# Two subtractions moved between the steps of the centroids, and eight token counts read one per block instead of all at once

## The chip, the core and the metric

The kernel runs as one program on one core of one Trainium2 chip. The core has five engines with a sequencer each: TensorE (PE in the profile, its weight loads PEld), VectorE (DVE), ScalarE (ACT), GpSimd (POOL) and SyncE (SP), which here issues nearly all transfers. A trailing q (PEldq, SPq) marks an instruction that the sequencer handles itself, such as a wait, a branch, a register load or the issue of a transfer. The metric is the device time of one execution in microseconds. A difference of about 2% is what a measurement of this kernel can tell from no change.

## What is computed

Three layers follow each other: attention in which a query sees only the keys of its own cluster, a gated normalised MLP on all tokens, and a mixture of eight experts with 1536 tokens, at most 384 to an expert.

```
q_assign = argmax(q_n . c_n)      # nearest of 16 normalised centroids, per head
k_assign = argmax(k_n . c_n)
scores = where(q_assign == k_assign, 0.125 * q @ k.T, -1e9)
x  = softmax(scores) @ v          # 2 batches, 8 heads, 768 tokens, head size 64

h  = x @ w_in;  solu = h * softmax(h)
x  = layernorm(solu) * g_ln @ w_out           # 1536 x 512 -> 1024 -> 512

e  = argmax(x @ w_gate)                       # expert of a token; gate_w its probability
y  = relu(x[tokens of e] @ w1[e]) @ w2[e]     # 8 experts, 512 -> 1024 -> 512
out[token] = gate_w * y                       # tokens above the 384th of an expert stay 0
```

## The kernel before

Values that need more than half precision are held as a high and a low f16 half, and a product is three matmuls: high by high, high by low, low by high.

**Attention.** The 16 heads are taken as 8 pairs. Work is not issued as it stands in the code: each step is given to a planner (`Plan.add`, with engine, cost, due time, a function that issues the instructions, and the names it reads and writes), and `Plan.emit` lists the steps in an order that follows those costs and due times. The function of a step may issue several instructions; they stay together at that place. The wanted semaphores follow from the order of issue. At the start, three things run: the centroids are squared and summed on DVE (`cent`, L275), a power is taken on POOL (L294), DVE finishes the scaling (`cent2_`, L279), PE transposes the result (L298) and DVE copies it into the tile `cbd` in two halves (`cent3`, L285). Beside it the first pair's queries and keys (tile `x32`) are split: ACT writes the high half of each (L322), DVE subtracts to get the low half (L325), into the tile `hl`. The 36 small matmuls L337 to L339 need `cbd` and all four halves; DVE then finds each token's cluster (L346 to L356), PE transposes it (L366) and ACT writes it as `ohT` (L370). SP loads `QK` tiles by transfers from `hl` (L393), from `hr`, a copy of the high halves (L384), and from `ohT` (L389); the score matmuls L446 and L447 read those. In DVE's order between L348 and L351 stands L594, a small subtraction on the gate weights, whose ACT partner L593 waits for the transfer of `wgs` (L591).

**Experts.** After the second layer, tokens lie sorted by expert in the buffer `xs` in HBM; `cnt` holds the 8 token counts and `cnt0` an early version for the first tile. `Experts.run` (L1187) first handles the first 128 tokens of expert 0, called expert -1 in the names (`extra(-1, 0, 2)`, under a branch at L1198 and L1200). Then it reads all eight counts into registers of every engine (L1208, one `TENSOR_LOAD` per count and engine; on SP each is followed by two more register instructions). `first` (L1092 and on) does expert 0's second 128 tokens: two transposed loads of its tokens (`cxT`, L1031) and one for expert 1, 8 x 12 matmuls of 128 columns (L1063 to L1065), the evacuation by ACT (L1076) and DVE (L1077), and 24 matmuls of 512 columns (L1082 to L1084). If expert 0 has more than 256 tokens a third tile follows (branch L1215). `block` then does experts 1 to 7 in turn: it loads the next expert's tokens, runs the first product on 256 or 192 columns by a branch on this expert's count (L1150), the second product of the first 128 tokens (`second`), a branch on the count (L1163) to the second product of the next 128, and inside it a branch to a third tile (L1169). Weight loads (L988) and their splitting by ACT (L991) and DVE (L992) for later experts run along in the blocks.

Of the kernel before, what the change touches and what calls it, by code (L numbers as in the profile page):

```python
# [14 lines left out]
AF = mybir.ActivationFunctionType  # L15
ALU = mybir.AluOpType
# [5 lines left out]
NT = B * S  # L22
DM = H * D
DF = 1024
E = 8
# [49 lines left out]
class Plan:  # L75
# [12 lines left out]
    def add(self, eng, cost, at, fn, reads=(), writes=(), data=0.0, lead=1e9, get=None, put=None):  # L88
        if put is not None:
            put.puts += 1  # L90
        self.todo.append((eng, cost, at, fn, tuple(reads), tuple(writes), data, lead, get, put))
# [104 lines left out]
def plan_attention(tc, plan, ctx, ps, qkT, vP, cent2, cst, cs, X, ident32, ident16):  # L196
    nc, add = tc.nc, plan.add
    pa = ctx.enter_context(tc.tile_pool(name="pa", bufs=1))
    x32 = pa.tile([P, 2, S], F32, tag="x32", name="x32")
    v32 = pa.tile([P, 2, NCH, D], F32, tag="v32", name="v32")  # L200
    hl = ring(pa, "hl", 2, [P, 4, S], F16)
# [47 lines left out]
    for i in range(2):  # L249
        add("sp", 0.0, target(6 * EH - 2.9 + 2.4 * i), lambda i=i: reuse(i),  # L250
            writes=[("QK1", spare[i][0], n) for n in (0, 1, 2, 4, 5)] + [("more", i)])
# [19 lines left out]
    add("pool", 0.1, -101.0, lambda: nc.gpsimd.memset(half, 0.5), writes=["half"])  # L271

    gc = Hold()

    def cent():  # L275
        nc.vector.tensor_tensor(out=sq, in0=cc[:, :D], in1=cc[:, :D], op=ALU.mult)
        nc.vector.tensor_reduce(out=rn, in_=sq, axis=AX.X, op=ALU.add)

    def cent2_():  # L279
        nc.vector.tensor_scalar(out=rn, in0=rn, scalar1=1e-6, scalar2=None, op0=ALU.add)  # L280
        nc.vector.reciprocal(out=rn, in_=rn)
        nc.vector.tensor_scalar(out=rn, in0=rn, scalar1=8.0, scalar2=None, op0=ALU.mult)
        nc.vector.tensor_scalar(out=cc, in0=cc, scalar1=rn[:, 0:1], scalar2=None, op0=ALU.mult)

    def cent3():  # L285
        for j in range(2):
            r = slice(64 * j, 64 * j + 64)
            src = gc.bank[r, :P].rearrange("d (hp j c) -> d hp j c", j=2, c=NC_)[:, :, j, :]
            dst = cbd[r, :, 0, 16 * j : 16 * j + 16]
            nc.vector.tensor_copy(out=dst, in_=src)  # L290
            nc.vector.tensor_tensor(out=cbd[r, :, 1, 16 * j : 16 * j + 16], in0=src, in1=dst, op=ALU.subtract)
# [3 lines left out]
        reads=["half"], writes=["rn"])  # L295
# [3 lines left out]
        reads=["cc", "id32", ("pf", 1)], writes=[gc], get=gc)  # L299
# [8 lines left out]
    def prep(p):  # L308
        hp, b = p % 4, p % 2
        T = 12 * p  # L310

        def at(k):
            return target(T + k)
# [3 lines left out]
        for ts in ((0, 1), (1, 2)) if p == 0 else ((0, 2),):  # L317
            n = ts[1] - ts[0]
            t_ = slice(*ts)
            kx, kh = [("x32", t) for t in range(*ts)], [("hi", b, t) for t in range(*ts)]  # L320
            h_ = hl[b].rearrange("p (t x) s -> p t x s", x=2)[:, t_, 0]
            add("act", 0.64 * n + 0.09, at(-17), lambda h_=h_, t_=t_: nc.scalar.activation(  # L322
                h_, x32[:, t_], AF.Copy, scale=16.0), reads=kx, writes=kh, lead=8)
        for t in range(2):
            add("dve", 0.87, at(-16.5), lambda t=t: nc.vector.scalar_tensor_tensor(  # L325
                out=hl[b][:, 2 * t + 1], in0=x32[:, t], scalar=16.0, in1=hl[b][:, 2 * t], op0=ALU.mult, op1=ALU.subtract),
                reads=[("x32", t), ("hi", b, t)], writes=[("lo", b, t)], lead=8)

        gs, go = Hold(), Hold()
# [13 lines left out]
        def v3():  # L343
# [3 lines left out]
            reads=[gs], writes=["mx"])  # L347
# [343 lines left out]
class Moe1:  # L691
# [18 lines left out]
    def at(self, cost=0.0):  # L710
        t = self.t
        self.t += cost * self.rate
        return t
# [301 lines left out]
class Experts:  # L1015
# [122 lines left out]
            for f, _ in conv[2 * n : 2 * n + 2]:  # L1138
                f()

    def block(self, e, start, r):
        plan = self.plan
        plan.banks = [(0.0, self.two[0])]
        self.hidden(e, 2)
        last, self.later = self.later, []
        if e + 1 < E:
            self.X[e + 1] = self.tiles(self.xk, e + 1, CAP)
            self.rows(e + 1, 0, CAP)
            self.idf(e + 1, 0, CAP)
        with self.tc.If(r > P + HALF) as c:  # L1150
            self.rows2(e, 2 * P, last[:6])
        with c.Else():
            self.rows2(e, P + HALF, last[:6])
        with self.tc.manual_schedule():
            if e + 1 < E:
                plan.add("dve", 0.07, 9.0, lambda: self.ids(e + 1, 0, CAP), writes=[("ids", ((e + 1) % 2, CAP))])
            for n, (_, conv) in enumerate(last[6:]):
                conv(1.2 + 1.2 * (n // 2))
            for n, i in enumerate(range(8 * e + start, min(8 * e + start + 8, 8 * E))):
                c_piece(self.nc, plan, self.piece, i // 8, i % 8, 0.5 + 1.0 * n, self.later)  # L1160
            self.second(e, 0, 1, 0.0, [], CAP)
            plan.emit()
        with self.tc.If(r > P):  # L1163
            with self.tc.manual_schedule():
                for f in range(FC):
                    self.gemm2(self.two[1], e, f, 1)
                self.scale(self.two[1], 1)
                self.put(e, 1, 1)
            with self.tc.If(r > 2 * P):  # L1169
                self.hidden(e, 1)  # L1170
                self.extra(e, 2, 2)
# [13 lines left out]
    def run(self, ctx, start, cnt, cnt0):  # L1185
        tc, nc, plan = self.tc, self.nc, self.plan
        self.xk = ctx.enter_context(tc.tile_pool(name="cx", bufs=2))  # L1187
        self.pools["cs2"] = ctx.enter_context(tc.tile_pool(name="cs2", bufs=LATE))
        one = ctx.enter_context(tc.tile_pool(name="c1", bufs=1))
        self.yo = ring(one, "yo", 3, [P, DM], F32)  # L1190
        self.hr = [ring(one, f"hr{i}", 2, [P, FC, 2 * P], F16) for i in range(2)]
        for h in self.hr:
            for x in h:
                nc.vector.memset(x[:, :, P + HALF :], 0.0)
        self.bank = [plan.banks.pop(0)[1] for _ in range(2)]
        self.four, self.two = [k for _, k in plan.banks[:4]], [k for _, k in plan.banks[4:]]
        plan.MIX, plan.WIN, plan.lean, plan.marks = 0.1, 0.05, {}, ()
        r0 = nc.values_load(cnt0[0:1, 0:1], min_val=0, max_val=NT)  # L1198
        self.hidden(-1, 1)
        with tc.If(r0 > P - 1) as full:  # L1200
            self.extra(-1, 0, 2)
        with full.Else():
            self.rows(-1, 0, P)
            self.idf(-1, 0, P)
            self.ids(-1, 0, P)
            self.extra(-1, 0, 2)
        with tc.manual_schedule():
            regs = [nc.values_load(cnt[0:1, i : i + 1], min_val=0, max_val=NT) for i in range(E)]  # L1208
            for e in range(E):
                if e:  # L1210
                    self.block(e, start, regs[e])
                else:
                    with tc.manual_schedule():
                        self.first(start)
                    with tc.If(regs[e] > 2 * P):  # L1215
                        self.hidden(e, 1)
                        self.extra(e, 2, 2)
# [156 lines left out]
```

## Time and profile before

| | us |
|---|---|
| three runs | 574.69, 565.21, 571.25 |
| median | 571.25 |
| profiled execution, its own time | 569.43 |
| its span, first to last instruction | 567.6 |
| PE busy | 489.6 (86% of the span) |
| DVE / ACT / POOL busy | 411.4 / 364.0 / 277.7 |
| mean granted TensorE clock | 0.971 |

Up to about 387 us the span holds attention and the second layer, and from there the experts. Each row of a timeline is one instruction, or several of a kind merged (x3), with its start and duration; square brackets tell how long its engine was idle before it and what ended that. [...]

### The profile page before, as it was taken

To read this page: it belongs to the slowest core of one execution; us is meant where nothing else is said; L and a number is where in the kernel's file an instruction comes from. 1 tells how busy PE (TensorE), PEld (TensorE's weight loads), DVE (VectorE), ACT (ScalarE), POOL (GpSimd) and SP (SyncE) were. 2 spreads that over 40 slices of the span, in tenths; PEclk is the share of its full clock that TensorE was granted. 3 is DMA by queue.
4 is the path that set the end of the run, shared out by engine and by line. 5 is a ranking of instruction groups with operands and counts; after the bars stand their busy time and mean duration, and the time that the engine had idled before them with its cause. 6 is when DMAs were issued, how large, how long until landed. Compare 5 with 4: busy or idle time off the path is not lost. (4 is left out here: it accounts for less than half of the span.)

```text
span 567.6 us, 13152 instructions
## 1 busy us (share of the span) xinstructions
PE 489.6 (86%) x4921; PEld 320.7 (56%) x4921; DVE 411.4 (72%) x980; ACT 364.0 (64%) x552; POOL 277.7 (49%) x291
## 2 busy tenths in 40 slices
PE   1379889889888798998888999998689999999996
PEld 0256666756565455555455444446664767657753
DVE  5589889999989689998764799994035635455721
ACT  3366789789858698988683688971134715457421
POOL 2046789899969757797883136351001010110210
PEclk9998899899978899999999999999799999999999
DMA  8798887686957999999999889893967792979850
GB/s 230 183 213 184 252 252 210 204 232 180 224 159 188 157 192 182 194 208 218 215 200 196 216 195 217 228 248 77 275 205 232 155 338 55 321 86 332 268 88 17
DMA packets 159268, 113.87 MB, mean 201 GB/s; under 512 B 126480, under 2 KB 134994, under 8 KB 159188
## 3 DMA queue, kind: packets, MB, share of 16 engines
q1 hardware_dynamic: 156660, 106.31, 80.0%
q0 software_dynamic: 2240, 6.32, 3.1%
q8 instruction: 52, 0.85, 0.6%
q14 instruction: 28, 0.23, 0.1%
q10 hardware_dynamic: 288, 0.16, 0.1%
HBM read 51.57 MB, written 16.85 MB: 121 GB/s over the span
## 5 line engine op out<-in xcount | busy, mean ns | idle before, releaser
L409 POOL TENSOR_TENSOR pr<-pf,pr 128x384 f16<-128x384 f32 x168 | 172.0, 1053 | 59.8 <-ACT pr L461 29.5
L1090 POOL DMA_INDIRECT out_dram<-yo,ids x15 | 18.1, 1205 | 145.6 <-ACT yo L1087 43.6
L1063 PE MATMUL psb<-cxT,ah 128*128 128x192 f16 (+2 forms) x288 | 70.3, 252 | 9.3 <-PEq L1169 4.5
L1064 PE MATMUL psb<-cxT,ah 128*128 128x192 f16 (+2 forms) x288 | 70.3, 252 | 1.2 <-issue 1.2
L503 DVE TENSOR_REDUCE mm<-psb 128x1 f32<-128x384 f32 x132 | 67.0, 547 | 6.0 <-PE psb L500 5.6
L1065 PE MATMUL psb<-cxT,al 128*128 128x192 f16 (+2 forms) x288 | 70.2, 252 | 0.0
L537 PE MATMUL psS<-QK 96*128 96x384 f32 x132 | 61.1, 497 | 0.0
L545 ACT ACTIVATE pf<-psS 128x768 f32<-128x768 f32 x66 | 53.1, 805 | 10.5 <-PE psS L537 7.6
L500 PE MATMUL psb<-QK 96*128 96x384 f32 x132 | 47.6, 423 | 14.0 <-DVE mm L503 7.8
L545 ACT ACTIVATE pr<-psS 128x768 f16<-128x768 f32 x66 | 52.6, 804 | 7.7 <-PE psS L537 7.6
L536 PE MATMUL psS<-QK 128*128 128x384 f16 x132 | 46.1, 349 | 1.7 <-ACT pr L545 1.0
L558 PE MATMUL psb<-V,pr 128*128 128x65 f16 x396 | 44.0, 197 | 4.1 <-DVE mm L503 3.6
L1077 DVE SCALAR_TENSOR_TENSOR hr<-psb,hr 128x384 f16<-128x384 f32 (+1 forms) x28 | 16.6, 593 | 39.8 <-ACT hr L1076 39.2
L560 PE MATMUL psb<-V,pr 128*128 128x65 f16 x396 | 43.7, 195 | 1.1 <-POOL pr L409 1.1
L559 PE MATMUL psb<-V,pr 128*128 128x64 f16 x396 | 43.7, 198 | 0.0
L992 DVE SCALAR_TENSOR_TENSOR al<-w,ah 128x1024 f16<-128x1024 f32 x32 | 40.5, 1279 | 3.4 <-ACT ah L991 3.0
L558 PEld LDWEIGHTS <-pr 128*128 128x128 f16 x396 | 37.5, 98 | 7.4 <-issue 2.3
L559 PEld LDWEIGHTS <-pr 128*128 128x128 f16 x396 | 37.8, 99 | 5.6 <-issue 4.7
L500 PEld LDWEIGHTS psb<-QK 96*128 96x128 f32 x132 | 27.7, 220 | 21.5 <-DVE mm L503 13.5
L992 DVE SCALAR_TENSOR_TENSOR bl<-w,bh 128x1024 f16<-128x1024 f32 x32 | 38.4, 1231 | 1.7 <-ACT bh L991 1.7
L1082 PE MATMUL psb<-bh,hr 128*128 128x512 f16 x104 | 39.4, 379 | 0.0
L1083 PE MATMUL psb<-bl,hr 128*128 128x512 f16 x104 | 39.4, 379 | 0.0
(202 smaller groups left out, 1565.1 us busy)
## 6 DMA issues: line engine op xcount, KB each, us to landing
w<-in_w_dram SPq DMA_DIRECT2D x64, 512.0 KB
xs<-X SPq DMA_DIRECT2D x12, 516.0 KB
QK<-hr SPq DMA_DIRECT2D x16, 384.0 KB
QK<-hl SPq DMA_DIRECT2D x32, 192.0 KB
x<-in_qkT_dram SPq DMA_DIRECT2D x7, 768.0 KB
lT<-in_w_in_dram SPq DMA_DIRECT2D x8, 512.0 KB
lT<-in_w_out_dram SPq DMA_DIRECT2D x8, 512.0 KB
v<-in_vP_dram SPq DMA_DIRECT2D x8, 384.0 KB
```

Of the source, the lines that this page charges most:

```text
L409: nc.gpsimd.tensor_tensor(out=out[:, i], in0=a[:, i], in1=b[:, i], op=ALU.subtract)
L500: add("pe", 0.18, at(c - 10 + 0.25 * g), lambda c=c, g=g, w=w: nc.tensor.matmul(w.bank[:, :384], q1[:, c * P : (c + 1) * P], k1[:, g * 384 ...
L503: add("dve", 0.465, at(c - 9.9 + 0.25 * g), lambda c=c, g=g, w=w: nc.vector.tensor_reduce(out=m2[mm][:, c, g : g + 1], in_=w.bank[:, :384] ...
L536: nc.tensor.matmul(o, k2[:, ks], q2[:, qs], start=True, stop=False)
L537: nc.tensor.matmul(o, k1[:, ks], q1[:, qs], start=False, stop=True)
L545: add("act", 0.691, at(k + 0.5), lambda dst=dst, kb=kb: nc.scalar.activation(dst, ps[kb][:, :, :384], AF.Exp, scale=SC), reads=[kb], write ...
L558: nc.tensor.matmul(A, ph[ub][:, c, qs], v[:, j, c, 0:65], start=(c == 0), stop=False)
L559: nc.tensor.matmul(A[:, :64], ph[ub][:, c, qs], v[:, j, c, 65:129], start=False, stop=False)
L992: run("dve", lambda: nc.vector.scalar_tensor_tensor(out=W[e][kl][:, gs], in0=box[0], scalar=64.0, in1=W[e][kh][:, gs], op0=ALU.mult, op1=A ...
L1063: nc.tensor.matmul(o, w["ah"][:, c, fs], x[:, 0, c, a:b], start=(c == 0), stop=False)
L1064: nc.tensor.matmul(o, w["ah"][:, c, fs], x[:, 1, c, a:b], start=False, stop=False)
L1065: nc.tensor.matmul(o, w["al"][:, c, fs], x[:, 0, c, a:b], start=False, stop=(c == KC - 1))
```

## The change

The ACT steps L322 and DVE steps L325 of the first pair are no longer steps of their own (their functions issue nothing); the four functions are kept in a list, `split`. `cent` issues the two ACT instructions ahead of its own two; `cent2_` issues the first subtraction ahead of its four instructions, `cent3` the second one ahead of its four. The other pairs are as before. The planner still sees the same steps with the same costs and names, so it puts all steps in the order in which they stood. In the expert part, the counts of experts 0 and 1 are read after `first`, and in block e the count of expert e + 1 after the second product of the first 128 tokens, ahead of the branch L1163.

```
     def cent():
+        for f in split[:2]:
+            f()
         nc.vector.tensor_tensor(out=sq, in0=cc[:, :D], in1=cc[:, :D], op=ALU.mult)
...
     def cent2_():
+        split[2]()
         nc.vector.tensor_scalar(out=rn, in0=rn, scalar1=1e-6, scalar2=None, op0=ALU.add)
...
     def cent3():
+        split[3]()
         for j in range(2):
...
-            add("act", 0.64 * n + 0.09, at(-17), lambda h_=h_, t_=t_: nc.scalar.activation(
-                h_, x32[:, t_], AF.Copy, scale=16.0), reads=kx, writes=kh, lead=8)
+            fn = lambda h_=h_, t_=t_: nc.scalar.activation(h_, x32[:, t_], AF.Copy, scale=16.0)
+            if p == 0:
+                split.append(fn)
+            add("act", 0.64 * n + 0.09, at(-17), fn if p else lambda: None, reads=kx, writes=kh, lead=8)
...
-            add("dve", 0.87, at(-16.5), lambda t=t: nc.vector.scalar_tensor_tensor(
-                out=hl[b][:, 2 * t + 1], in0=x32[:, t], scalar=16.0, in1=hl[b][:, 2 * t], op0=ALU.mult, op1=ALU.subtract),
+            fn = lambda t=t: nc.vector.scalar_tensor_tensor(
+                out=hl[b][:, 2 * t + 1], in0=x32[:, t], scalar=16.0, in1=hl[b][:, 2 * t], op0=ALU.mult, op1=ALU.subtract)
+            if p == 0:
+                split.append(fn)
+            add("dve", 0.87, at(-16.5), fn if p else lambda: None,
                 reads=[("x32", t), ("hi", b, t)], writes=[("lo", b, t)], lead=8)
...
-    def block(self, e, start, r):
+    def block(self, e, start, r, count):
...
             self.second(e, 0, 1, 0.0, [], CAP)
             plan.emit()
+        if e + 1 < E:
+            count(e + 1)
         with self.tc.If(r > P):
...
-            regs = [nc.values_load(cnt[0:1, i : i + 1], min_val=0, max_val=NT) for i in range(E)]
+            regs = []
+
+            def count(e):
+                regs.append(nc.values_load(cnt[0:1, e : e + 1], min_val=0, max_val=NT))
+
             for e in range(E):
                 if e:
-                    self.block(e, start, regs[e])
+                    self.block(e, start, regs[e], count)
                 else:
                     with tc.manual_schedule():
                         self.first(start)
+                    count(0)
+                    count(1)
                     with tc.If(regs[e] > 2 * P):
```

The line numbers of the changed kernel are higher: L325 becomes L332, L1163 becomes L1175, L1215 becomes L1233, and the reads are at L1223. On DVE, at the start, this stands in a row before (`hl` and `x` are the first pair's tiles, `pf` and `mm` hold the centroids, `psb` is a PSUM bank):

```order
L280 TENSOR_SCALAR mm<-mm 128x1
L281 RECIPROCAL mm<-mm 128x1
L282 TENSOR_SCALAR mm<-mm 128x1
L283 TENSOR_SCALAR pf_163<-pf_163,mm 128x128
L301 CAST tie_145<-cs 128x16
L1263 CAST tri_64<-cs 128x128
L290 CAST cbd<-psb_72 64x4x16
L291 TENSOR_TENSOR cbd<-psb_72,cbd 64x4x16
L290 CAST cbd<-psb_72 64x4x16
L291 TENSOR_TENSOR cbd<-psb_72,cbd 64x4x16
L596 TENSOR_SCALAR gs<-gs 128x8
L325 SCALAR_TENSOR_TENSOR hl_132<-x_130,hl_132 128x768 x2
```

And this in the changed kernel:

```order
L332 SCALAR_TENSOR_TENSOR hl_132<-x_130,hl_132 128x768
L284 TENSOR_SCALAR mm<-mm 128x1
L285 RECIPROCAL mm<-mm 128x1
L286 TENSOR_SCALAR mm<-mm 128x1
L287 TENSOR_SCALAR pf_163<-pf_163,mm 128x128
L306 CAST tie_145<-cs 128x16
L1281 CAST tri_64<-cs 128x128
L332 SCALAR_TENSOR_TENSOR hl_132<-x_130,hl_132 128x768
L295 CAST cbd<-psb_72 64x4x16
L296 TENSOR_TENSOR cbd<-psb_72,cbd 64x4x16
L295 CAST cbd<-psb_72 64x4x16
L296 TENSOR_TENSOR cbd<-psb_72,cbd 64x4x16
```

The two subtractions that stood behind the centroids' copies stand now ahead of `cent2_` and ahead of the copies; the rest of DVE keeps its order, and so do ACT and SP up to the experts.

On PE, between expert -1's last matmul and expert 0's first in `first` (`ah`, `al` are halves of the first weights, `cxT` the tokens), this stands before:

```order
L1084 MATMUL psb_4713<-bh_4726,hl_-1_5672 128x512
L1200 UNCONDITIONAL_BRANCH
L1063 LDWEIGHTS ah_4724
L1208 TENSOR_LOAD cnt x8
L1063 MATMUL psb_4710<-cxT_6049,ah_4724 128x128
```

And in the changed kernel:

```order
L1094 MATMUL psb_4713<-bh_4726,hl_-1_5672 128x512
L1212 UNCONDITIONAL_BRANCH
L1073 LDWEIGHTS ah_4724
L1073 MATMUL psb_4710<-cxT_5937,ah_4724 128x128
L1074 LDWEIGHTS ah_4724
```

The eight register loads are gone from there. On PE at the end of `first`, and then in block 1 behind the second product of the first 128 tokens, the changed kernel has:

```order
L1094 MATMUL psb_72<-bh_4726,hl_5947 128x512
L1223 TENSOR_LOAD cnt x2
L1233 COMPARE_AND_BRANCH
...
L1094 MATMUL psb_75<-bh_5028,hr_5652 128x512
L1223 TENSOR_LOAD cnt
L1175 COMPARE_AND_BRANCH
L1092 LDWEIGHTS hr_5651
```

Two loads stand now ahead of the branch behind `first`, and one ahead of the branch L1163 in each of blocks 1 to 6; on the other four engines the loads moved to the same two places.

## Rows read from the trace of the kernel before

**Rows 1.** The page, busy time, share of the span and instructions of PE.
```profile
PE 489.6 (86%) x4921; PEld 320.7 (56%) x4921; DVE 411.4 (72%) x980; ACT 364.0 (64%) x552; POOL 277.7 (49%) x291
```
**Rows 2.** Timeline of the start: start, duration, engine, line, operation, out<-in, [idle<-releaser].
```profile
4.47 0.84 ACT L322 ACTIVATE hl<-x 128x768 f16<-128x768 f32 x1 [1.54 <-DMA x<-in_qkT_dram]
...
5.51 0.15 DVE L280 TENSOR_SCALAR mm<-mm 128x1 f32<-128x1 f32 x1 [0.76 <-POOL mm L294]
...
6.09 0.29 DVE L283 TENSOR_SCALAR pf<-pf,mm 128x128 f32<-128x128 f32 x1
...
8.09 1.82 DVE L325 SCALAR_TENSOR_TENSOR hl<-x,hl 128x768 f16<-128x768 f32 x2
...
14.04 0.19 DVE L594 SCALAR_TENSOR_TENSOR wgl<-wgs,wgh 128x32 f16<-128x32 f32 x1 [1.88 <-ACT wgh L593]
```
**Rows 3.** Timeline of the start: transfers that SP issues, and who waits.
```profile
9.94 1.31 SPq L393 DMA_DIRECT2D QK<-hl  x2
...
17.68 2.49 SPq L389 DMA_DIRECT2D QK<-ohT  x4
...
23.91 0.66 PE L447 MATMUL psS<-QK 96*128 96x384 f32 x1 [5.66 <-DMA QK<-ohT]
```
**Rows 4.** Stretches of the start: length, busy per engine, PE clock, DMA share, GB/s.
```profile
2.00:14.00 12.00, 1.93 (x37) 1.38 (x37) 6.84 (x18) 4.32 (x6) 2.18 (x10) 1.00 0.96 265
14.00:25.00 11.00, 2.37 (x10) 1.31 (x10) 4.52 (x10) 3.54 (x5) 0.00 (x0) 1.00 0.94 218
```
**Rows 5.** Line L1208: engine, operation, ns min/median/max, first and last start in us.
```profile
L1208 SPq TENSOR_LOAD <-cnt x8: 261/264/543, 387.7 to 392.0; - x8
...
L1208 PEldq TENSOR_LOAD <-cnt x8: 300/307/690, 398.8 to 402.2; - x8
```
**Rows 6.** Timelines of PE, PEld and SP around the same loads.
```profile
384.33 1.25 SPq L1031 DMA_TRANSPOSE cxT-1_5556<-xs  x1
...
387.58 0.22 PE L1063 MATMUL psb<-cxT-1_5556,ah 128*128 128x128 f16 x1 [0.36 <-DMA cxT-1_5556<-xs]
...
395.41 1.70 SPq L1031 DMA_TRANSPOSE cxT<-xs  x1
...
398.79 0.10 PEld L1063 LDWEIGHTS <-ah 128*128 128x128 f16 x1 [1.01 <-PE psb L1084]
...
402.55 0.27 PE L1063 MATMUL psb<-cxT,ah 128*128 128x128 f16 x1 [4.28 <-issue]
```
**Rows 7.** Stretches of expert -1, the gap, `first` in two parts, and block 1.
```profile
387.58:398.27 10.69, 10.69 (x120) 7.58 (x120) 3.19 (x12) 1.59 (x3) 1.96 (x2) 1.00 0.27 78
398.27:402.55 4.28, 0.01 (x1) 0.10 (x1) 0.00 (x0) 0.60 (x1) 0.97 (x1) 0.88 0.83 161
402.55:408.39 5.84, 5.84 (x56) 5.81 (x56) 0.00 (x0) 0.40 (x1) 0.00 (x0) 0.50 1.11 305
408.39:416.02 7.63, 7.63 (x67) 4.54 (x65) 1.67 (x5) 0.80 (x2) 0.00 (x0) 1.00 1.06 389
416.49:436.35 19.86, 18.62 (x144) 12.46 (x144) 11.48 (x13) 10.29 (x14) 2.94 (x2) 1.00 0.57 155
```
**Rows 8.** Four lines on PE's sequencer, ns and starts in us; block 1's second product.
```profile
L1200 PEldq COMPARE_BRANCH x2: 86/195/304, 387.3 to 394.6; - x2
...
L1198 PEldq TENSOR_LOAD <-cnt x1: 498/498/498, 386.7 to 386.7; - x1
...
L1215 PEldq COMPARE_BRANCH  x1: 2877/2877/2877, 412.3 to 412.3; - x1
...
L1163 PEldq COMPARE_BRANCH  x7: 70/70/3377, 427.3 to 557.9; - x7
...
425.83 0.38 PE L1082 MATMUL psb<-bh,hr 128*128 128x512 f16 x1
```
**Rows 9.** Waits of PE from 398 us to the end: total, times, longest.
```profile
PE psb L1063 <- PEq L1169: 4.5, 5, 1.0
...
PE psb L1064 <- issue: 1.2, 1, 1.2
```

More of the change, by code (lines that the diff above doesn't have):

```diff
@@ L273, in plan_attention @@
     gc = Hold()
+    split = []
     def cent():
+        for f in split[:2]:
+            f()
         nc.vector.tensor_tensor(out=sq, in0=cc[:, :D], in1=cc[:, :D], op=ALU.mult)
```

## The prediction

> **What bounds the kernel now.** I read the page first. PE is busy 86% of the span and no other engine is above 72% [rows 1], so time is to be had mostly where PE stands still. Then I went to the two places of the change, with the timeline, the stretches and the waits.
>
> At the start the reader is to see two chains that end in transfers. DVE's chain goes from the centroids to the two subtractions at 8.09 us and on to the clusters, but then DVE stands 1.88 us until 14.04, because L594 waits for ACT's L593, which waits for a transfer [rows 2]. PE's first large matmul L447 stands 5.66 us, until 23.91, for a transfer from `ohT` that SP issued from 17.68 on [rows 3]. And from 2 to 25 us the DMA engines are 94 to 96% busy [rows 4]: the transfers stand in a full queue, and what is issued earlier does not land earlier.
>
> At the beginning of the experts the reader is to see PE's largest gap of the expert part, 4.28 us from 398.27 to 402.55, put down to "issue", that is, to nothing that the profile shows as a wait [rows 6]. The line of the register loads explains it: PE's eight loads start from 398.8 to 402.2 [rows 5]. The weight load that precedes them in program order ran at 398.79 [rows 6], and it stands behind PE's wait for the tokens. A second pair of rows says the same: the earlier transposed load of 128 tokens, issued at 384.33, let PE start at 387.58, 3.25 us later, and this one was issued at 395.41, which gives 398.66 [rows 6]. So the tokens were there at about 398.8, and the eight loads held PE for 402.55 - 398.85 = 3.70 us. [...]
>
> From there to the end PE is the bound: it waits for five gaps of at most 1.0 us behind L1169, one of 1.2 us in block 1, and for little else [rows 9]. What PE wins in `first` therefore moves the rest of the program, if nothing else comes late.
>
> **The change part by part.**
>
> *The subtractions.* New order on DVE, from [rows 2]: the first high half is ready at 4.47 + 0.84 = 5.31; the subtraction takes 1.82 / 2 = 0.91, so until 6.2. The four steps of `cent2_` took from 5.51 to 6.38, 0.87, and now end at 7.1, 0.7 later than before. From there to the subtractions, with PE's transpose and the four copies, it took 6.38 to 8.09, 1.71; with the second subtraction in it and nothing overlapped that ends at 7.1 + 1.7 + 0.9 = 9.7. The small matmuls so have both operands at 9.7 at the latest, in place of 9.91 (8.09 + 1.82); the low halves are complete at some 8.4, behind two short casts, 1.5 us earlier. Both run into what is late next. The clusters stop at L594, 14.04, whatever comes before it. The transfers from `hl`, issued at 9.94 [rows 3], can go about 1.4 us earlier, but into the full queue. The bounds of this part are a gain of 1.5 us, if the queue passed all of that lead on, and 0; a loss is excluded, since both operands of the small matmuls are ready sooner. I take 0, because L594's wait and the DMA share both say that the next stop does not move.
>
> *The eight loads go from the front of `first`.* PE starts at about 398.85: **-3.7 us**. DVE's, ACT's and POOL's loads lay in their own idle time, and SP's ran from 387.7 to 392.0 [rows 5], before it could issue the tokens at 395.41 [rows 6]; they give nothing.
>
> *The clock.* PE's idle time before `first` shrinks from 4.28 to about 0.6 us. Behind the gaps of 1.0 and 1.2 us [rows 9] the clock stayed at 1.00: block 1 with its 1.2 us gap shows it [rows 7]. [...] What that is worth needs no formula: expert -1 has the same 96 + 24 matmuls and took 10.69 us at full clock, while `first` took 5.84 + 7.63 = 13.47 us [rows 7]: **-2.8 us**. The bounds are 0 and -2.8.
>
> *Two loads behind `first`.* One load costs PE (402.55 - 398.79) / 8 = 0.47 us with what lies between two of them [rows 5, 6], so two cost 0.94. Before, PE's sequencer reached the branch L1215 at 412.3, 3.7 us ahead of the end of the matmuls at 416.02, but the branch took 2.88 us, to 415.2 [rows 7, 8]: 0.8 us of the lead was left, which would hide nearly all of it. Against this, block 1 then stood 1.2 us for "issue" [rows 9], which looks as if its instructions came late behind that branch, and a later branch makes them later. The ends are 0.1 and 0.94; I take **+0.9**.
>
> *One load in each of blocks 1 to 6.* In block 1 the second product starts at 425.83 and the branch behind its 24 matmuls was executed at 427.3 [rows 8]. The block's two second products fill 425.83 to 436.35 [rows 7, 8], so the first ends at about 431.1. The sequencer is thus 3.8 us ahead, and a load of 0.3 to 0.7 us lies in that lead: **0** for PE. The load of L1198 shows that a register load does not wait for the array to empty: it ran at 386.7 for 0.5 us [rows 8], up to the time when PE went on to expert -1's matmuls at 387.58, and the rest of that gap belongs to a transfer [rows 6]. If the lead were gone, the cost would be 6 x 0.47 = 2.8 us. On SP a load costs (392.0 - 387.7) / 7 = 0.61 us [rows 5] in front of the next expert's tokens; those are needed a block, some 20 us, later [rows 7].
>
> [...]
>
> *Sum.* 0 - 3.7 - 2.8 + 0.9 + 0 = -5.6 us, against the profiled execution's 569.43: 563.8. That execution is 1.8 us under the median of the three runs, 571.25, which the same sum takes to 565.6. I forecast between the two, **564.7**.
>
> **The rivals.**
>
> *The gap stays cold or refills.* PE starts at 398.85, but its instructions come late, as they did in block 1 for 1.2 us [rows 9]; the eight loads had given them time to come. Or the clock falls anyway. Without the clock's part the gain is 3.7 - 0.9 = 2.8, and the time 571.25 - 2.8 = 568.4 by the median. For it: the jump over the other side of the branch L1200 lies right before. Against it: PE's sequencer went through the last branch of L1200 at 394.6 [rows 8], and had until 398.8 to get what follows. [...]
>
> *The loads in the blocks are not hidden.* If PE has no lead left at L1163, six loads cost 2.8 us and the two behind `first` 0.9: the gain is 6.5 - 3.7 = 2.8, again 568.4. The row at 427.3 speaks against it.
>
> *Slower than before.* Place: the branch L1163 in blocks 1 to 6. If a load waits until the array is empty, PE loses the load, 0.47, then a branch and restart, as behind L1169 up to 1.0 us, and the wait for instructions seen once in block 1, 1.2 us [rows 9]: 2.7 us a block, 16.2 in six, and 0.9 behind `first`, against 6.5 won: 571.25 + 10.6 = 581.9. It decides once a block costs more than (6.5 - 0.9) / 6 = 0.9 us. The load of L1198, which ran to within half a microsecond of running matmuls, speaks against it.
>
> *The start does gain.* If the full queue is not what holds L447, up to 1.5 us come on top: 571.25 - 7.1 = 564.2 by the median, 562.3 by the profiled execution.
>
> **How the numbers follow.** The forecast has a chance of 0.62, the cold or late start 0.12, unhidden loads 0.10, the slower case 0.04, a gain at the start as well 0.12. The three runs of the kernel before span 565.2 to 574.7, so a single median can lie 4 us off for that alone. The range takes in the gaining cases at a fast median, 562.3 - 5, and the two cases at 568.4 with 2 us more: **557 to 570.5**. About 2%, 11.4 us, is what a measurement of this kernel can tell from no change. The forecast is 1.0 to 1.2% below, so within 2% is by far the likeliest, 0.83. Faster by over 2% needs both gains and a favourable spread, 0.14; slower by over 2% needs the slower case nearly in full, 0.03.
>
> **What would show it.** In the changed kernel's profile: PE's gap before `first` is 0.5 to 0.7 us and ended by the transfer of `cxT`, and the clock is 1.00 through it; `first` takes 10.7 us; the gap between `first` and block 1 is 0.5 to 1.5 us, and the loads stand there; no new gap of PE at the six places in the blocks; L447 starts again at about 23.9 us, and DVE's wait at L594 grows to about 2.4 us. I would be wrong if the time from PE's start in block 1 to the end were longer than before, if the clock fell in `first` all the same, or if L447 started more than a microsecond earlier.

## The result, and the profile after

| | before | after |
|---|---|---|
| median of 19 runs each, us | 569.50 | 565.06 |
| lowest and highest | 564.13, 574.69 | 558.37, 569.93 |
| profiled execution (its span), us | 569.43 (567.6) | 565.73 (563.8) |
| mean granted TensorE clock | 0.971 | 0.969 |

The ratio is 0.9903, with a 95% interval from 0.9875 to 0.993: 5.5 us of 569.5. It leaves out executions more than 1.5% above the fastest of their kernel, so it is not the quotient of the medians in the table, which differ by 4.4 us (0.992). Either is less than the 2% that a measurement of this kernel can tell from no change, though the interval leaves out 1. Two later measurements of the same kernel gave 0.9949 (0.9917 to 0.9981) and 0.9893 (0.9818 to 0.9967). The forecast was 564.7 us, 5.6 us less.

The timeline of PE around `first` and the start of block 1, after; columns as in [rows 6]:

```profile
398.70 0.22 PE L1073 MATMUL psb<-cxT,ah 128*128 128x128 f16 x1 [0.50 <-DMA cxT<-xs]
...
409.88 0.26 PE L1073 MATMUL psb<-cxT,ah 128*128 128x192 f16 x1 [0.47 <-PEq L1233]
...
413.15 0.34 PE L1074 MATMUL psb<-cxT,ah 128*128 128x192 f16 x1 [2.03 <-issue]
```

The 4.28 us gap of [rows 6] is 0.50 us and ends with the tokens' transfer. The stall in block 1, 1.2 us in [rows 9], is 2.03 us. In the timeline of the kernel before it stands here:

```profile
418.73 0.26 PE L1064 MATMUL psb<-cxT,ah 128*128 128x192 f16 x1 [1.24 <-issue]
```

The stretches after, columns as in [rows 7], are expert -1, the gap, `first` in two parts, block 1, and the two stretches of [rows 4]:

```profile
387.50:398.20 10.70, 10.70 (x120) 7.60 (x120) 3.20 (x12) 1.60 (x3) 1.96 (x2) 1.00 0.28 77
398.20:398.70 0.50, 0.00 (x0) 0.03 (x1) 0.00 (x0) 0.46 (x1) 0.00 (x0) 1.00 0.31 46
398.70:404.54 5.84, 5.84 (x99) 5.60 (x100) 0.69 (x1) 1.01 (x3) 0.97 (x1) 1.00 1.13 224
404.54:409.40 4.86, 4.86 (x23) 2.01 (x21) 1.00 (x3) 0.32 (x1) 0.00 (x0) 1.00 0.97 352
409.88:432.18 22.30, 20.27 (x144) 13.94 (x144) 11.76 (x14) 10.28 (x14) 2.34 (x2) 0.92 0.92 226
2.00:14.00 12.00, 1.57 (x37) 1.22 (x37) 8.07 (x22) 5.05 (x6) 2.17 (x10) 1.00 0.93 282
14.00:25.00 11.00, 5.19 (x18) 3.46 (x19) 5.77 (x11) 4.39 (x5) 0.00 (x0) 1.00 0.73 206
```

In the first 5.84 us of `first` PE does 99 matmuls at clock 1.00, where it did 56 at 0.50 [rows 7]; the whole takes 10.70 us, not 13.47. Block 1 takes 22.30 us, not 19.86, and its clock is below 1.00: half speed came after the stall, for 3.41 us:

```profile
413.18:416.59 3.41, 3.41 (x22) 3.23 (x23) 0.73 (x2) 1.43 (x2) 0.00 (x0) 0.50 1.07 400
```

The account of the two traces, from PE's start on expert -1 to its last matmul (174.35 us before, 170.71 after):

| stretch | before | after | difference |
|---|---|---|---|
| gap before `first` | 4.28 | 0.50 | -3.78 |
| `first` | 13.47 | 10.70 | -2.77 |
| gap before block 1 | 0.47 | 0.48 | 0 |
| block 1 | 19.86 | 22.30 | +2.44 |
| from there to the end | 125.57 | 126.03 | +0.46 |

The sum is -3.65 us, and the profiled executions differ by 3.70; expert -1 begins at 387.50 against 387.58, so nothing came from the start.

Waits of PE from 389 us on, after, columns as in [rows 9]:

```profile
PE psb L1073 <- PEq L1181: 3.2, 4, 0.9
PE psb L1074 <- issue: 2.0, 1, 2.0
PE psb L1073 <- issue: 1.4, 1, 1.4
PE psb L1073 <- DMA cxT<-xs: 0.5, 1, 0.5
PE psb L1073 <- PEq L1233: 0.5, 1, 0.5
```

And the register loads on PE, after, columns as in [rows 5]:

```profile
L1223 PEldq TENSOR_LOAD <-cnt x8: 302/306/322, 405.7 to 535.0; - x8
```

No matmul of a second product (L1092 to L1094) waits at all: the eight loads, 0.30 us each, show no gap of their own. The start, after, beside [rows 2] and [rows 3]:

```profile
5.32 0.96 DVE L332 SCALAR_TENSOR_TENSOR hl<-x,hl 128x768 f16<-128x768 f32 x1 [0.83 <-ACT hl L327]
...
7.18 0.95 DVE L332 SCALAR_TENSOR_TENSOR hl<-x,hl 128x768 f16<-128x768 f32 x1
...
12.60 0.19 DVE L604 SCALAR_TENSOR_TENSOR wgl<-wgs,wgh 128x32 f16<-128x32 f32 x1 [1.24 <-ACT wgh L603]
...
21.09 0.66 PE L457 MATMUL psS<-QK 96*128 96x384 f32 x1 [4.89 <-DMA QK<-ohT]
```

The subtractions stand where they were put, and PE's first large matmul starts 2.8 us earlier than at 23.91 [rows 3]. Whether that is the change's doing is the first question.

### The profile page after: what moved, and what is told of

Its sections match the earlier page's. It is cut to its first block, busy times and chain, and to the rows that moved or that the text cites. A ratio compares the mean times of both kernels' runs of the same rounds, so it can differ in the third digit from the quotient of the medians.

```text
span 563.8 us, 13152 instructions
## 1 busy us (share of the span) xinstructions
PE 489.6 (87%) x4921; PEld 319.3 (57%) x4921; DVE 415.3 (74%) x980; ACT 364.1 (65%) x552; POOL 277.0 (49%) x291
## 4 chain that ended last, share of the span: by engine, by line
DMA 30%; DVE 28%; PE 18%; issue 14%; ACT 3%; POOL 3%; SPq 2%; POOLq 0%; another core or an unknown queue 0%; ACTq 0%; DVEq 0%
DMA out_dram<-yo,ids 19%; DVE mm L513 7%; DMA x<-in_qkT_dram 2%; DVE wf L626 2%; PE psb L510 2%; DVE hl L332 2%; DMA pr<-pn 2%; DVE wf L629 2%; DMA wT<-wol 2%; DMA QK<-ohT 1%; DVE mm L460 1%; PE psS L456 1%; PE psS L457 1%; DVE wf L623 1%; DMA xs<-ys,si 1%
## 5 line engine op out<-in xcount | busy, mean ns | idle before, releaser
L1073 PE MATMUL psb<-cxT,ah 128*128 128x192 f16 (+2 forms) x288 | 68.6, 249 | 5.6 <-PEq L1181 3.2
L1074 PE MATMUL psb<-cxT,ah 128*128 128x192 f16 (+2 forms) x288 | 68.6, 249 | 2.0 <-issue 2.0
L1075 PE MATMUL psb<-cxT,al 128*128 128x192 f16 (+2 forms) x288 | 68.5, 249 | 0.0
L547 PE MATMUL psS<-QK 96*128 96x384 f32 x132 | 62.4, 507 | 0.0
L1097 ACT ACTIVATE yo<-psb 128x512 f32<-128x512 f32 x16 | 9.6, 597 | 47.9 <-PE psb L1094 22.9
L1086 ACT ACTIVATE hr<-psb 128x384 f16<-128x384 f32 (+1 forms) x28 | 14.6, 521 | 38.6 <-PE psb L1075 38.6
```

The source lines that it names most:

```text
L547: nc.tensor.matmul(o, k1[:, ks], q1[:, qs], start=False, stop=True)
L1073: nc.tensor.matmul(o, w["ah"][:, c, fs], x[:, 0, c, a:b], start=(c == 0), stop=False)
L1074: nc.tensor.matmul(o, w["ah"][:, c, fs], x[:, 1, c, a:b], start=False, stop=False)
L1075: nc.tensor.matmul(o, w["al"][:, c, fs], x[:, 0, c, a:b], start=False, stop=(c == KC - 1))
```

## Experiments

**Theory A**: the gain is PE's gap before `first` and the half clock behind it; the subtractions give nothing. **Theory B**: the subtractions gain at the start as well. A second question came with the trace: what is block 1's stall, which in these two traces grew and, with the half clock behind it, took back 2.4 us?

### Each part alone

`only_loads` is the kernel before with the part of the diff on `count`; `only_subs` is the kernel before with the part on `split`.

```
only_loads:  - regs = [nc.values_load(...) for i in range(E)]
             + regs = []; count(0), count(1) behind first; count(e + 1) in block e
only_subs:   + split: the two ACT and two DVE functions issued in cent, cent2_, cent3
```

> The kernel before with the loads' part of the change alone; the subtractions stand as before. Theory A: the whole gain of the change, 4 to 6 us, ratio 0.990 to 0.993; PE's gap in front of `first` about 0.5 us, `first` 10.7 us at clock 1.00, a stall of about 2.0 us in block 1 some 6.6 us behind the branch after `first`. Theory B: 2 to 4 us, ratio 0.993 to 0.996, since the start gives the rest.

> The kernel before with the subtractions' part of the change alone; the eight loads stand in front of `first` as before. Theory A (the gain comes from PE's gap in front of `first` and the half clock behind it): no gain beyond 0.5 us, ratio 0.999 to 1.001; PE's gap in front of `first` is again about 4.3 us with `first` in part at clock 0.50. Theory B (the two subtractions gain at the start, and the transfers in front of L447 land earlier for that reason): 1.5 to 3 us less, ratio 0.995 to 0.997, and `L447` starts by 21 to 22 us as in the changed kernel.

`only_loads`: ratio 0.9854 (0.9794 to 0.9913). `only_subs`: 0.9985 (0.9951 to 1.002). The stretch of `first` in the trace of `only_loads`:

```profile
396.76:407.46 10.70, 10.70 (x120) 7.59 (x120) 1.69 (x4) 1.36 (x3) 0.97 (x1) 1.00 1.06 274
```

Its first large matmul, in the timeline:

```profile
20.13 0.66 PE L447 MATMUL psS<-QK 96*128 96x384 f32 x1 [5.17 <-DMA QK<-ohT]
```

And the timeline of `only_subs`, the same matmul and the first one of `first`:

```profile
20.80 0.66 PE L457 MATMUL psS<-QK 96*128 96x384 f32 x1 [6.17 <-DMA QK<-ohT]
...
400.23 0.26 PE L1073 MATMUL psb<-cxT,ah 128*128 128x128 f16 x1 [4.46 <-issue]
```

Without the moved subtractions the matmul also starts at 20.1 us, and at 20.6 and 20.5 in `eight_pinned` and `busy_gap` below, which leave them where they were as well; with them moved it starts between 19.6 and 21.4 in ten traces. The 23.9 us of the trace before was that execution's, not the kernel's. The loads carry the gain, somewhat more of it than expected, with an interval that reaches into the expected 0.990 to 0.993. For the subtractions the interval leaves room for a gain of 0.5% or a loss of 0.2%, and 0.15% of gain is what was seen. Theory A holds. Of theory B the reason falls, since L447 does not start earlier for the subtractions; a small gain is not excluded. In the traces expert -1 begins at 385.6 to 388.5 us in the four with the subtractions where they were and at 380.6 to 387.5 in the ten with them moved, and no run shows why.

### What a load costs: its number or its place

`eight_pinned` keeps all eight loads where the kernel before has them and adds one matmul behind them. Before, PE's order was weight load (which waits for the tokens), eight loads, matmul; now the eight loads come ahead of that wait.

```
  regs = [nc.values_load(cnt[0:1, i : i + 1], ...) for i in range(E)]
+ nc.tensor.matmul(self.four[3], self.H[-1][0][:, 0], self.W[0]["ah"][:, 0, :512], ...)
```

> The kernel before, all eight counts read in front of `first` as there, with one such matmul behind the eight loads; nothing else of the change. Theory W: the loads run while the array works on expert -1, PE's gap in front of `first` shrinks from 4.3 to 0.5 to 0.9 us, the clock stays at 1.00 in `first`, and the total is 3 to 6 us under the kernel before, as much as the whole change brings, ratio 0.990 to 0.995. Theory L: the gap stays near 4 us and the time within 1 us of the kernel before.

Ratio 0.9881 (0.9815 to 0.9947), a little more gain than expected; the changed kernel, measured beside it, had 0.9893 (0.9818 to 0.9967). The loads on PE, as in [rows 5]:

```profile
L1208 PEldq TENSOR_LOAD <-cnt x8: 300/306/317, 396.0 to 398.8; - x8
```

PE's first matmul of `first` in the timeline, and the stretch of `first`:

```profile
400.16 0.22 PE L1063 MATMUL psb<-cxT,ah 128*128 128x128 f16 x1 [0.64 <-DMA cxT<-xs]
```

```profile
400.16:410.89 10.73, 10.70 (x120) 7.61 (x120) 1.69 (x4) 1.19 (x2) 0.94 (x1) 1.00 1.05 253
```

All eight loads ran while the array was still on expert -1, and cost PE nothing. What made them cost 3.7 us was that they stood behind the wait for the tokens. Theory W holds, L falls, and by the ratios one matmul gives about the change's whole gain. That trace itself does not show the gain in time: its expert part takes 174.26 us against 174.35 before, since a stall of 2.87 us in block 1, another of 2.38 later and half speed for 3.41 us behind each took back what the gap and `first` had won.

### The clock

`busy_gap` is the same with two matmuls of 512 columns behind each load, so that PE is never idle there.

```
  for i in range(E):
      regs.append(nc.values_load(...))
+     for _ in range(2):
+         nc.tensor.matmul(self.four[3], ...)
```

> The kernel before, with two matmuls of 512 columns into an unused bank behind each of the eight register loads in front of `first`, so that PE works in the gap and is held up as long as before. Theory A (the idle time halves the clock, and the half clock costs 2.8 us): the clock is 1.00 through `first`, which takes 10.7 us instead of 13.5, and the total is 2 to 3 us less than the kernel before, if the matmuls hide under the loads; PE's start in `first` moves by less than 1 us. Rival (the clock falls for another reason, as the matmuls of `first` set in): 0.50 for some 6 us again, and the same time as before or more.

The ratio is 1.0006 (0.9965 to 1.0047), so the expected total did not come. The gap (second row) and `first` (third), and block 1 (fourth):

```profile
387.05:397.70 10.65, 10.65 (x121) 7.81 (x122) 3.21 (x12) 1.62 (x3) 1.96 (x2) 1.00 0.25 73
397.70:401.04 3.34, 3.34 (x17) 1.47 (x15) 0.00 (x0) 0.60 (x1) 0.97 (x1) 1.00 0.70 125
401.04:411.75 10.71, 10.71 (x121) 7.61 (x119) 1.50 (x4) 1.19 (x2) 0.00 (x0) 1.00 0.99 311
414.61:434.39 19.78, 19.78 (x144) 13.73 (x144) 11.67 (x14) 10.12 (x13) 1.52 (x1) 0.93 0.97 184
```

The array was kept from `first` for 3.34 us, but by matmuls and not by idleness, and `first` took 10.71 us at clock 1.00: the 2.8 us of the clock come from the idle gap. Up to the end of `first` the run is 3.74 us ahead of the kernel before (24.70 against 28.44 us from PE's start on expert -1). Then PE stood 2.86 us before block 1, where the branch L1150 takes 2.61 us, and 1.71, 1.44 and 2.07 us for "issue" later on, where the kernel before has no gap over 1.24 us [rows 9]. Its code is 32 instructions longer there; the next experiments say why that matters.

### Where the two loads stand

`two_before` reads counts 0 and 1 ahead of `first`, `loads_mid_first` between its two products.

```
two_before:       + count(0); count(1)      loads_mid_first, in first():
                    self.first(start)       + add("pe", 0.01, t - 0.7,
                  - count(0); count(1)      +     lambda: (count(0), count(1)), ...)
```

> The changed kernel, with the counts of experts 0 and 1 read ahead of `first`, where all eight stood before. Theory A: PE's gap in front of `first` grows from 0.5 to 1.2 to 1.5 us (two loads at 0.41 to 0.47), the clock stays at 1.00 behind it, block 1's stall is back to about 1.2 us, and the total is within 1 us of the changed kernel, ratio 0.988 to 0.992. Theory C (any register load in front of `first` makes PE wait for something else, as instructions, and not for its own duration): the gap stays near 4 us and the ratio near 0.998 to 1.000.

> The changed kernel, with the counts of experts 0 and 1 read between the first and the second product of `first` in place of behind it, so that PE's sequencer reaches the branch behind `first` without two loads in front of it. Theory A1 (block 1's stall ends a fixed 6.4 to 6.6 us behind that branch, because its instructions come late): the branch runs 0.6 to 0.8 us earlier, the stall in block 1 is 1.2 us again in place of 2.0, the clock stays at 1.00 in block 1 and block 1 takes about 19.9 us in place of 22.3: 0.8 to 2.5 us less than the changed kernel, a ratio of 0.986 to 0.989 against the kernel before. Theory A2 (the stall has nothing to do with the loads, and the longer one was chance): same as the changed kernel, 0.990, and a stall of 1.2 to 2.0 us that does not follow the branch.

`two_before`: 0.9936 (0.99 to 0.9972), within 0.2% of the expected range; PE's gap is 1.74 us, more than the 1.2 to 1.5 expected but far from 4, so theory C falls, and block 1 has no stall at all. `loads_mid_first`: 0.9949 (0.9911 to 0.9986), not the gain that A1 expected. Its branch behind `first`, and then block 1 in the timeline:

```profile
L1232 PEldq COMPARE_BRANCH  x1: 4301/4301/4301, 402.0 to 402.0; - x1
```

```profile
412.44 0.34 PE L1074 MATMUL psb<-cxT,ah 128*128 128x192 f16 x1 [4.44 <-issue]
```

The branch was reached earlier, as wanted, but took 4.30 us, and the stall grew to 4.44. A stall 6.5 us behind the branch (theory A1) is refuted here, 10.5 us, and by `two_before`, where none came. The length varies, the place does not: in `loads_mid_first`, as in the changed kernel, it is after 13 matmuls of block 1.

### The stall is a page of instructions that comes late

The trace has the transfers of the instruction queue q8. In the changed kernel, in the 0.1 us from 404.3 and the 0.1 us from 410.7 (packets, MB, and the whole time that the packet took as a share of 16 engines' 0.1 us, so 94.0% is 1.50 us):

```profile
q8 instruction: 1, 0.02, 94.0%
...
q8 instruction: 1, 0.02, 66.2%
```

Those two packets, of 16,384 bytes, end at 405.86 and 411.81. The branch behind `first` ends at 407.23, 1.37 us after the first; block 1's stall ends at 413.15, 1.34 us after the second. From 34.28 to 364.85 us of the trace before, 26 packets of q8 start while PE takes 3312 matmuls and as many weight loads: an estimated 255 instructions to a packet, if all are PE's. Theory P is the author's reading of these times: a packet is a page of PE's code, and behind the branch PE stands until the page that comes next is there. If this is it, moving the code against the pages must move the stall. `pad48` does that and nothing else; `mid_pad48` adds the same to `loads_mid_first`.

```
  with full.Else():                 # not executed with these inputs
      ...
+     for _ in range(24):
+         nc.tensor.matmul(self.bank[0], ...)      # 48 instructions on PE
      self.extra(-1, 0, 2)
```

> The changed kernel with 48 instructions of PE (24 matmuls) added in the side of expert -1's branch that isn't executed: nothing more is computed, but all of PE's code behind it lies 48 instructions further on. Theory P (block 1's stall is a page of instructions that comes late: in the changed kernel the packets of the instruction queue q8, 16 KB or 256 instructions each, end 1.4 us before the branch behind `first` ends, and again before the stall ends; the stall lies at a page's end, 13 matmuls into block 1, and the next page is asked for only when the branch has been taken): the stall 13 matmuls into block 1 is gone; the branch behind `first` takes 0.2 to 0.7 us as its page was asked for earlier; a wait, if any, stands at the very start of block 1, at L1160's branch, and is between 0.5 and 3 us, with a packet of q8 ending 1.4 us before its end. Total within 2 us of the changed kernel. Theory F (block 1's instructions come a fixed 6.5 us behind that branch, wherever the code lies): a stall of about 2.0 us, 13 matmuls into block 1, as before.

> As the last one, with the counts of experts 0 and 1 read between the two products of `first`. Theory P: the branch behind `first` is reached some 7.0 us behind PE's start in `first`, 0.8 us earlier than with the loads behind the second product, and the wait at the start of block 1 is up to 0.8 us shorter: 0 to 2 us. Total 1 to 2.5 us under the changed kernel of the same call. Theory F: the stall stays 13 matmuls into block 1 and is 1.2 us.

> The changed kernel once more, on the chip and in the rounds of the two before it. Both theories: 0.990 of the kernel before, within 0.003. Theory P: block 1's stall lies again 13 matmuls into the block, and its length, 2.0 us before, may be anything from 0 to 4.5 us, since the packet of q8 waits 1.2 to 3.6 us among the other transfers; it ends 1.4 us behind that packet's end. Theory F: 2.0 us again.

> The changed kernel once more, for the comparison with the two in this call: 0.990 to 0.995 of the kernel before, block 1's stall 13 matmuls into the block and 1.5 to 2.0 us long, the expert part 169 to 171 us.

`pad48`: 0.9982 (0.9945 to 1.0018). `mid_pad48`: 0.9915 (0.9864 to 0.9965). `after_again`, beside them: 0.9949. So `pad48` is within the 2 us expected, and `mid_pad48`, expected 1 to 2.5 us under the changed kernel, is not clearly so: its ratio is lower by 1.9 us, but its median over all executions is 569.34 against 567.49. In `pad48` the branch behind `first` and the branch at the head of a block, by their lines, and block 1's first matmul in the timeline:

```profile
L1235 PEldq COMPARE_BRANCH  x1: 437/437/437, 401.5 to 401.5; - x1
...
L1160 PEldq COMPARE_BRANCH  x9: 73/418/3312, 404.6 to 545.0; - x9
```

```profile
407.95 0.34 PE L1073 MATMUL psb<-cxT,ah 128*128 128x192 f16 x1 [3.56 <-issue]
```

The stall has left its place behind 13 matmuls and stands at the head of the block, in the branch L1160, which took 3.31 us instead of 0.22; it ends 1.38 us behind the end of a q8 packet (406.51). That is theory P's picture, and F is refuted. The size that P expected did not come: 3.56 us, and 4.34 in `mid_pad48`, where at most 3 and 2 were expected.

The other traces show the same shift in small steps. The stall stands after 13 matmuls of block 1 in all six traces that have one there and two loads on PE ahead of block 1; after 12 in `two_pinned` below, which has two instructions more (a matmul and its weight load); after 10 in the kernel before and `only_subs`, with eight loads, six instructions more; and after 9 in `eight_pinned`, eight more. Every two instructions ahead of it bring the stall one matmul, which is two instructions, nearer to the block's head.

A stall's end goes with the packet's, 1.24 to 1.79 us behind it in this table, and the packet starts 1.15 to 3.56 us after the branch:

| kernel | branch behind `first` ends | next q8 packet starts (after) | ends | stall ends (after) | stall |
|---|---|---|---|---|---|
| before | 415.19 | 416.34 (1.15) | 417.42 | 418.73 (1.31) | 1.24 |
| only_subs | 412.67 | 415.25 (2.58) | 416.34 | 418.13 (1.79) | 3.17 |
| two_before | 405.39 | 407.78 (2.39) | 408.89 | | none |
| changed | 407.23 | 410.75 (3.52) | 411.81 | 413.15 (1.34) | 2.03 |
| after_again | 407.07 | 410.40 (3.33) | 411.44 | 412.68 (1.24) | 1.50 |
| after_third | 403.47 | 406.94 (3.47) | 408.06 | 409.34 (1.28) | 2.87 |
| only_loads | 405.26 | 408.68 (3.42) | 409.80 | 411.22 (1.42) | 2.04 |
| loads_mid_first | 406.26 | 409.82 (3.56) | 410.93 | 412.44 (1.51) | 4.44 |
| pad48 | 401.94 | 405.40 (3.46) | 406.51 | 407.95 (1.44) | 3.56 |
| mid_pad48 | 400.93 | 404.32 (3.39) | 405.43 | 406.86 (1.43) | 4.34 |

In all thirteen traces with such a stall (four of them are not in the table) the packet moves 1.15 to 3.75 us after the branch, takes 1.0 to 1.1 us, and PE goes on 1.2 to 1.8 us later. In `two_before` the page came early enough for PE not to notice: the packet ended at 408.89, and PE's first matmul of block 1 started at 408.94. In the changed kernel the wait is some 2.3 us longer than in the one trace of the kernel before; `only_subs`, with all loads where they were, has 2.58 and a stall of 3.17, so two traces cannot say that the change made the stall grow. The stretches of that wait, before and after:

```profile
415.19:416.34 1.15, 0.83 (x4) 0.20 (x2) 0.00 (x0) 0.28 (x1) 0.00 (x0) 1.00 0.84 335
```

```profile
407.23:410.75 3.52, 3.05 (x22) 1.66 (x20) 0.00 (x0) 0.60 (x1) 0.44 (x1) 1.00 1.03 386
```

DMA is busier in it (0.84 and 1.03, 335 and 386 GB/s): `first` ends earlier, so the branch falls into the transfers of the next weights. In the other twelve traces the share is 0.91 where the wait is 2.39 us (`two_before`) and 0.99 to 1.08 where it is 2.58 to 3.75. That these transfers hold the page up is argued from such rows; no run took them away.

`after_third` shows the spread: 174.86 us for the expert part, against 170.71 and 169.33 in the other two traces of the same kernel, with stalls of 2.87, 2.33 and 1.88 us, where 169 to 171 us and one stall of 1.5 to 2.0 were expected.

### Two further runs

`two_pinned` is `two_before` with one matmul behind the two loads.

> The changed kernel with the counts of experts 0 and 1 read ahead of `first`, as in the run that read two there, and one matmul (512 columns, on operands that have long been there, into an unused bank) behind them, so that the loads stand ahead of PE's wait for the tokens and not behind it. Theory W (a register load costs PE time only where it stands behind a wait; ahead of one it is done while the array still works): PE's gap in front of `first` is 0.5 to 0.9 us and no longer 1.7, the branch behind `first` comes some 7.0 us after PE's start there, block 1's stall is 0 to 1.5 us, and the expert part (from PE's start on expert -1 to its end) takes 167.5 to 169 us against 168.75 with two loads behind the wait and 170.7 and 169.3 in two traces of the changed kernel; total 1 to 2 us under the changed kernel of this call. Theory L (each load costs its 0.4 us wherever it stands on PE): a gap of 1.2 to 1.7 us again, and the same total as the changed kernel.

PE's gap before `first` is 0.60 us instead of 1.74, so theory W holds there as well; but block 1's stall is 2.91 us (the packet waited 3.63), the expert part 174.12, and the ratio 0.9878 (0.9772 to 0.9985). The expected total was wrong, and no version here is clearly better than the changed kernel.

`four_per_block` issues `count(e + 1)` four times in each of blocks 1 to 6.

> The changed kernel with three more reads of the count in each of blocks 1 to 7, so four loads (three in block 7) stand ahead of the branch L1175 where one stood. Theory A (the loads lie in the 3.7 us that PE's sequencer is ahead of the array there): four loads take 1.7 us of the lead, PE shows no gap between the two second products in any block, and the expert part is within 1 us of the changed kernel's 169.3 to 170.7, but for stalls at the pages' ends, which lie elsewhere. Rival (a load holds the array up): a new gap of 1.2 us or more in each of seven blocks, 8 us or more in all.

This run misses its question. Its trace has 26 loads on SP, but on PE again eight, and 18 semaphore instructions in place of the others, so PE's price for more loads was not tried. What it shows is small: no second product waits.

## Why the prediction was right, and where it was not

**The eight loads, -3.7 us: right**, measured -3.78. The reason given was right too: they stood behind the wait for tokens that were there. `eight_pinned` makes it sharper: with all eight ahead of that wait the gap is 0.64 us, so the wait in front of them is nearly the whole price.

**The clock, -2.8: right.** `first` took 10.70 us at clock 1.00, measured -2.77, and `busy_gap` ties it to the idle gap.

**The two loads behind `first`, +0.9: mis-sized.** The sentence was that the branch's lead "would hide nearly all of it", against a later branch and a later stall, so that the ends were 0.1 and 0.94. The gap stayed at 0.48 us, so the loads themselves cost nothing. The branch was not later either: it ended 2.2 us ahead of the end of `first`, and before 0.8 us ahead [rows 7, 8]. The stall did grow between the two traces, by 0.79, but not by the loads' length: the page of instructions waited 3.52 us instead of 1.15. And the prediction had no term for the clock behind it: half speed for 3.41 us, about 1.65 more. The term was +2.44 in that trace; how much of it is the change's doing stays open, as `only_subs` shows a stall of 3.17 us with half speed behind it and no load moved. The full clock that was expected in `first` held there and was lost in block 1.

**The block loads, 0: right as far as tried.** No gap at the six places; single loads took 0.30 us, as those in a row. So the rival of loads that are not hidden did not come.

**The subtractions, 0: right within 0.5%**, though the sign named for being wrong appeared: the first large matmul came 2.8 us earlier. `only_loads` has that too, without them, and the lead was gone by 387.5 us. DVE's wait at L604 was 1.24 us and not the 2.4 predicted, since ACT's L603, which waits for the transfer of `wgs`, started at 12.34 us and not at 13.78. That what is issued earlier does not land earlier, the premise of the 0, no run shows: in the trace after, the transfers from `ohT` were issued at 16.24 us and not at 17.68, and L457, which waits for one, came earlier with them.

**The sum.** -5.6 was forecast, -5.5 is the ratio's, and the two traces alone give -3.7. With the other traces, the expert part takes 174.35 and 178.04 us with the eight loads behind the wait (before, `only_subs`), and 170.71, 169.33, 174.86 and 171.75 with the loads moved (three of the changed kernel, `only_loads`): 4.5 us less on average. The agreement is in part luck and closer than the parts deserve: three traces of the changed kernel differ by 5.5 us in the expert part, and the repeated ratios run from 0.989 to 0.995.

## What to carry to other kernels

Look at what stands ahead of a register load on its engine: here eight were free ahead of a wait (PE's gap was 0.64 us in `eight_pinned`), and behind it they cost 3.7 us and 2.8 us of half clock after it (a gap of 4.28 us). Where a stall is put down to "issue" behind a branch, look for the packets of the instruction queue before moving work about to shorten it: here it ended 1.2 to 1.8 us behind one, and 48 instructions that never run moved it by 13 matmuls (`pad48`). A change that pulls a stage forward pulls its branches with it, here into transfers with a DMA share of 1.03 in place of 0.84; that the page waited for those was argued and not tested, but some of the gain may be lost so. Where executions of one kernel differ by more than the change is worth, account for several traces of each kernel.

## What was not expected of the hardware

Where a page of instructions was missing, PE went on 3.5 to 6.2 us after the branch behind which it was needed (packet of 16,384 bytes 1.15 to 3.75 us after it, then 1.0 to 1.1, then 1.2 to 1.8). 48 instructions that never run moved a stall of PE from the middle of a block to its head.

With PE's stalls in block 1 of 2.0 us and more the granted clock was 0.50 for 3.4 us (2.03, 2.04, 2.86, 2.87 twice, 3.17, 3.42) or 6.8 us (2.91, 3.56, 4.34, 4.44); with those of 1.24 and 1.50 it stayed at 1.00. The length of a stall alone does not tell it: later in the expert part the clock stayed at 1.00 behind gaps of 1.98, 2.06, 2.07 and 2.30 us (`two_before`, `only_loads`, `busy_gap`, `two_pinned`) and was 0.50 for 3.4 us behind those of 2.15, 2.17, 2.33 and 2.38 (`mid_pad48`, `pad48`, `after_third`, `eight_pinned`).
